# Scores of paired blocks as products on quarters of the TensorE array, with a new order of the work

## The chip, the cores and the metric

The kernel runs on one core of one Trainium2 chip. The metric is the device time of one execution in microseconds (us). Three runs of the kernel before took 713.99, 714.02 and 714.16 us; the median is 714.02.

## What is computed

Causal attention over a sliding window, then two feed-forward layers. There are 4 sequences of 576 positions, 8 heads of 64 dimensions, model width 512, inner widths 2048 and 1024; all in float32.

```python
def _attn_ref(q, k, v):                       # each (4, 8, 576, 64)
    scores = np.matmul(q, k.transpose(0, 1, 3, 2)) / np.sqrt(64)
    rel = pos[:, None] - pos[None, :]
    scores = np.where((rel >= 0) & (rel < 64), scores, -1e9)
    attn = softmax(scores)                    # the denominator + 1e-9
    return np.matmul(attn, v)
# x: (2304, 512), heads side by side
h = x @ w_in;  x = (h * tanh(softplus(h))) @ w_out      # 512 -> 2048 -> 512
h = x @ w_in2; y = h * softmax(h)                       # 512 -> 1024
y = layer_norm(y) * g_ln;  out = y @ w_out2             # 1024 -> 512
```

## The kernel before

**Attention.** A sequence is cut into 9 blocks of 64 queries, 36 blocks in all. With a window of 64, a block of queries sees 128 keys: those of the block before and its own. The first block of a sequence sees the first 128 keys of the sequence, under a mask of its own (`mask_0` instead of `mask_n`).

Two heads are handled together (`NP` = 4 head pairs). For each block the host lays q out as a 128 x 128 matrix with head 0 in the upper left 64 x 64 corner, head 1 in the lower right one, and zeros in the other two; k of the two heads lies one above the other on 128 partitions. One product of line 535 then gives a tile of 128 rows (64 queries of head 0, 64 of head 1) by 128 keys. Half of what the array multiplies is zeros.

The first 4 blocks (`N0`) go one at a time, with an arrangement of their own. The other 32 go in 16 pairs (n, n+1): `a_qk` makes 8 products into one PSUM tile `ps` of 128 x 8 x 128, index c*NP + p for block c and head pair p. For blocks below `NM` = 8 (the pairs 4 and 6) the mask is added on TensorE: a bf16 product behind each score product (line 541). For the other 14 pairs `a_scale` scales and adds the mask on VectorE (line 584), in two instructions where one of the two blocks begins a sequence. Then follow the maximum (`a_max`, line 590), the subtraction (`a_sub`), the exponential (`a_exp` or `a_exp1`), the sum and its inverse (`a_norm`), the multiplication (`a_mul`), eight transposes (`a_tr`, line 638), the copy out of PSUM (`a_pt`) and the product with v (`a_pv`, line 674), whose output goes into `xt`, the input of the first layer, as two float32r parts.

**Feed-forward.** Line 720 makes the first product (12 instructions for each of the 84 items: 4 chunks of the inner dimension and 3 terms of the split), lines 754 and 765 the second one (8 and 4). Lines 848 and 921 are those of the second layer, line 896 the transposes between them. The weights come as 64-bit words that are converted on the chip, on ScalarE, GpSimd and VectorE (lines 348 to 369, 283 to 303).

**Order.** Each engine works through its instructions in program order. A planner (`Schedule`) makes that order when the program is built: each step has a cost per engine and a due time, the constants at the head of the file (`ATT_AT`, `PRE_AT`, `FIRST_AT` and so on) set the due times, and among the steps that could start soon the one due first is taken. Where the planner foresees that TensorE has to wait for longer than 0.8 us, `bridge` puts products of zeros ahead of a step (line 511), and 42 of them stand at the very start.

Of the kernel before, what the change touches and what calls it, by code (L numbers as in the profile page):

```python
# [19 lines left out]
ALU = mybir.AluOpType  # L20
# [4 lines left out]
P = 128  # L25
BLK = 64
# [18 lines left out]
}  # L45


MISH_AT = (-1.318, -2.197, 0.491, 1.432, 3.462)
M2_AT = 6.081

ATT_AT = (-5.653, 0.076, 2.634, -1.153, 0.28, -0.274, 1.979, 3.176, 1.472, 3.319, 2.907, -2.355)

PRE_AT = (-2.332, 0.405, 5.908, -2.312, -3.229, 2.258, 7.674, 7.347, 5.474, 3.689, 2.895)
PRE_STEP = 9.088

B_AT = (-12.318, 7.278, 7.65, 20.217, 4.626, 12.227, 1.901, 15.948)

CONV_PRIO = (-7.642, 5.531, 5.959, -1.47, 2.491, 3.681)
Q_LEAD = 11.954
V_LEAD = -10.804  # L60
G_AT = 10.0
K0_LATER = 7.392
FIRST_AT = (-53.151, -34.692, -15.071)
W_STEP = 0.535
M4_LATER = 8.119
BESIDE_AT = ((4.321, 2.306), (2.079, 3.404), (4.273, 13.061), (-3.239, 4.798), (2.709, 9.741))
PATIENCE = 0.212
SLACK = 3.235
H_X2 = (0,)
PE_MASK = True  # L70
N_ACC = 8
# [11 lines left out]
class Schedule:  # L83
# [112 lines left out]
def attention_moe_solu(  # L196
# [12 lines left out]
    nc = tc.nc  # L209
    B, S, DM = v.shape  # L210
    NP = qk.shape[3]
# [8 lines left out]
    NBB = S // BLK  # L220
    NB = NT // BLK
    scale = 1.0 / float(D) ** 0.5
# [5 lines left out]
    N0 = GROUPS[0] // BLK // 2  # L228
# [15 lines left out]
    mask_n = const.tile([P, P], F32, name="mask_n")  # L244
    mask_0 = const.tile([P, P], F32, name="mask_0")
# [16 lines left out]
    def make_mask_n():  # L262
# [140 lines left out]
    n = GROUPS[0] // 2  # L403
# [12 lines left out]
    def pe_of(i):  # L416
        return 24 * ((its[i][3] - its[i][2]) / 2400 + 0.0134)
# [4 lines left out]
    pos = [0.0]  # L422
    for i in range(NI):
        beside = sum(n / (c - a) for a, c, n in besides if a <= i < c)
        pos.append(pos[-1] + (pe_of(i) + beside / 128 * 4.1) / 4.16)
    END = pos[NI]
    first_it = {}
    for i, it in enumerate(its):
# [25 lines left out]
    qt, kt, vt = {}, {}, {}  # L454
# [62 lines left out]

    s_t, pt_t = {}, {}

    def a_qk(n):  # L520
        early = n < N0
        ns = (n,) if early else (n, n + 1)
        if early:
            ps = ps_x2.tile([P, NP, P], F32, tag="x2", name="ps_s")
        else:
            ps = ps_a.tile([P, 2 * NP, P], F32, tag="a", name="ps_s")
        bridge(ps)
        r = room["r"]
# [15 lines left out]
        s_t[n] = ps  # L544

    def a_max0(n):
        ps = s_t[n]
# [29 lines left out]
    def a_scale(n):  # L577
        ps = s_t[n]
        s = at_p.tile([P, 2 * NP, P], F32, tag="s2", name="s", bufs=2)
        firsts = [i % NBB == 0 for i in (n, n + 1)]  # L580
# [82 lines left out]
    def a_pv(n):  # L663
        pt = pt_t.pop(n)
        if n < N0:
            ps, ns = ps_h.tile([P, NP, BLK], F32, tag="h", name="ps_o"), (n,)
        else:
            ps, ns = ps_a.tile([P, NP, 2 * BLK], F32, tag="a", name="ps_o"), (n, n + 1)
        bridge(ps)
        for c, m in enumerate(ns):  # L670
            for p in range(NP):
                for h in range(2):
                    r = slice(h * BLK, (h + 1) * BLK)
                    nc.tensor.matmul(  # L674
                        out=ps[r, p, c * BLK:(c + 1) * BLK],
                        lhsT=vt[m][:, (2 * p + h) * D:(2 * p + h + 1) * D],
                        rhs=pt[:, c * NP + p, r],
                        start=True, stop=True,
                    )
        x_t[n] = ps  # L680
# [119 lines left out]
    with tc.manual_schedule():  # L800
# [144 lines left out]
        masks_r = step(dict(act=0.2), -99, make_mask_r, ((2, mask_n),), after=[masks, q0], uses=[room_q])  # L945
        whole, split_of, first_hi = {}, {}, {}
        first_ld = []

# [34 lines left out]
        step(dict(pe=3.8), -200, warm_up, new=[warm], uses=[warm])  # L983


        x_of, xbuf, pv_of, pv_last = {}, {}, {}, []
        m1_of, m2_of, k0_of, v0_of = {}, {}, [], []

        def finish(n, t, offs, mu, bufs, O, cps):
            j, o = group_of[n]  # L990
            w, pt = bufs
            pv = step(dict(pe=0.648 * len(cps)), t + offs[0], a_pv, n, after=cps, new=[O], uses=[pt, O] + w)
            new = []
            if o == 0:
                xbuf[j] = Buf("xt")
                new = [xbuf[j]]
            k = len(cps)
            x = step(COSTS["x0" if k == 1 else "x"], t + offs[1], a_x, n, after=[pv], new=new, uses=[O])
            xl = step(dict(dve=0.42 if k == 1 else 0.69), t + offs[2], a_xl, n, after=[x], uses=[O])
            x_of[n] = xl  # L1000
            if n >= N0:
                x_of[n + 1] = xl
            pv_of[n] = pv
# [24 lines left out]
        def attend(n, t, offs, gate):  # L1028
            ks, ws, lks, lvs = [], [], [], []
            for m in (n, n + 1):  # L1030
                k, w = Buf("qk"), Buf("v")
# [5 lines left out]
            two = 2 if n % NBB and (n + 1) % NBB else 2.2  # L1037
            pv_of_old = pv_last[-2:-1]
            if n < NM:
                qk = step(dict(pe=2.2), t + offs[0], a_qk, n, after=lks + pv_of_old + [masks_r], new=[S], uses=ks + [S, room_q])  # L1040
# [15 lines left out]
            r = step(dict(dve=0.35), t + offs[5], a_norm, n, after=[sm], new=[rs], uses=[rs])  # L1056
# [58 lines left out]
        base = {}  # L1115
        for k, (i0, i1, _) in enumerate(besides):
            lo, hi = pos[i0] - BESIDE_AT[k][0], pos[i1] - BESIDE_AT[k][1]
            n0 = N0 if k == 0 else starts[k] // BLK
            nb = (starts[k] if k else 0) // BLK + GROUPS[k] // BLK - n0
            for b in range(0, nb, 2):  # L1120
                t = lo + b * (hi - lo) / nb
                i = max([i for i in range(NI) if pos[i] <= t - 1], default=-1)
                base.setdefault(i, []).append((n0 + b, t))
        for n, t in base.get(-1, []):
            attend(n, t, ATT_AT, [])
        for i in range(NI):
            mish(i)
            for n, t in base.get(i, []):
                attend(n, t, ATT_AT, [m1_of[i]] if i else [])


        attention_done = list(pv_of.values()) + list(x_of.values())
        ob = step(dict(none=0.0), 0, open_b, after=attention_done)
# [7 lines left out]
        for t in range(NTT):  # L1141
            j, o = tile_of[t]
            a = END + 2.2 + (t - 1) * UB
# [4 lines left out]
            h = Buf("b" + str(t % 2))  # L1148
# [77 lines left out]
```

## Time and profile before

| | |
|---|---|
| median of 3 runs | 714.02 us |
| span of the profiled execution | 713.9 us |
| TensorE busy | 704.2 us (99%) |
| VectorE busy | 385.5 us (54%) |
| ScalarE busy | 314.3 us (44%) |
| GpSimd busy | 44.0 us (6%) |
| mean granted TensorE clock | 0.996 |

The span runs from the first to the last instruction of one profiled execution; what lies around it is 0.1 us against the median. PE is TensorE's products, PEld its weight loads, DVE VectorE, ACT ScalarE. Products are pipelined, and their ends in the profile are modelled: for the pace of TensorE one reads from start to start. "Idle before" is the time in which an engine had nothing to do ahead of an instruction, with the instruction that ended the wait.

### The profile page before, as it was taken

The numbers are of one execution on the slowest core, as the hardware profiler recorded it, in microseconds if no ns is written. First come the engines' busy times: TensorE is split into PE (matmuls) and PEld (weight loads), VectorE is DVE, ScalarE is ACT, GpSimd is POOL, SyncE is SP. The second block draws the span as 40 slices with busy tenths as digits, with TensorE's granted clock in tenths as the row PEclk, the third lists the DMA queues.
The fourth block names the chain that finished last, engine by engine and source line by source line (L and its number), as shares of the span: only waits on it lengthen the run. The fifth ranks groups of instructions, "written<-read, shape, count | busy, mean of one in ns | idle before, by whom it ended". The sixth has DMA issues, their size and how long they took to land.

```text
span 713.9 us, 10238 instructions
## 1 busy us (share of the span) xinstructions
PE 704.2 (99%) x4180; PEld 613.0 (86%) x4180; DVE 385.5 (54%) x570; ACT 314.3 (44%) x536; POOL 44.0 (6%) x71
## 2 busy tenths in 40 slices
PE   9989999999999999999999999999999999999997
PEld 8889888888888888888899999999788888888886
DVE  4997988874362153443354113665656555555551
ACT  4878997554353242443354224654223332323221
POOL 2000010000000000000000100000212111111100
PEclk9999999999999999999999999999999999999999
DMA  8755756635117032022041104330111010101001
GB/s 299 277 207 177 266 163 221 236 118 177 60 45 221 0 98 95 15 89 89 1 148 45 31 1 157 124 118 16 60 44 60 31 59 30 60 29 60 16 29 45
DMA packets 37855, 71.71 MB, mean 100 GB/s; under 512 B 2864, under 2 KB 15152, under 8 KB 37808
## 3 DMA queue, kind: packets, MB, share of 16 engines
q1 hardware_dynamic: 37808, 71.06, 29.4%
q8 instruction: 33, 0.54, 0.3%
q14 instruction: 14, 0.11, 0.1%
HBM read 59.51 MB, written 11.53 MB: 100 GB/s over the span
## 4 chain that ended last, share of the span: by engine, by line
PE 93%; DVE 3%; ACT 2%; DMA 1%; SPq 0%; issue 0%; ACTq 0%
PE ps_h L720 26%; PE x L754 18%; PE h L848 14%; PE po L921 14%; PE x L765 9%; PE ps_s L535 5%; PE ps_o L674 2%; PE pt L896 2%; PE ps_t L638 2%; DMA room_q<-qk 1%; PE ps_t L511 1%; DVE st L369 0%; DVE w L303 0%; DVE nm L590 0%; DVE st L363 0%; DVE s L600 0%
## 5 line engine op out<-in xcount | busy, mean ns | idle before, releaser
L720 PE MATMUL ps_h<-xt,w 128*128 128x512 f32 (+2 forms) x1008 | 212.3, 360 | 0.5 <-ACT mc L730 0.4
L720 PEld LDWEIGHTS ps_h<-xt,w 128*128 128x128 f32 x1008 | 177.2, 188 | 21.9 <-ACT mc L730 0.6
L754 PE MATMUL x<-g,w 128*128 128x512 f32 (+2 forms) x672 | 149.0, 363 | 2.1 <-DVE w L287 1.3
L754 PEld LDWEIGHTS x<-g,w 128*128 128x128 f32 x672 | 118.5, 190 | 15.9 <-DVE w L287 1.4
L303 DVE SCALAR_TENSOR_TENSOR g<-mc,g 128x512 fp32r<-128x512 f32 (+2 forms) x84 | 51.5, 614 | 128.6 <-ACT g L283 127.7
L848 PE MATMUL h<-w,xs 128*128 128x512 f32 x432 | 104.7, 398 | 0.0
L921 PE MATMUL po<-w,lz 128*128 128x512 f32 x432 | 101.8, 391 | 0.7 <-ACT lz L902 0.7
L921 PEld LDWEIGHTS po<-w,lz 128*128 128x128 f32 x432 | 80.7, 188 | 17.9 <-ACT lz L902 0.9
L848 PEld LDWEIGHTS h<-w,xs 128*128 128x128 f32 x432 | 80.2, 188 | 18.3
L283 ACT ACTIVATE g<-mc 128x512 fp32r<-128x512 f32 (+2 forms) x72 | 41.6, 579 | 108.5 <-PE x L765 108.3
L730 ACT ACTIVATE mc<-ps_h 128x512 f32<-128x512 f32 (+2 forms) x84 | 45.0, 538 | 85.8 <-PE ps_h L720 77.6
L765 PE MATMUL x<-g,w 128*128 128x512 f32 (+2 forms) x336 | 80.4, 361 | 0.0
L765 PEld LDWEIGHTS x<-g,w 128*128 128x128 f32 x336 | 59.6, 188 | 6.7
L838 POOL TENSOR_TENSOR xs<-xr,xs 128x512 fp32r<-128x512 f32 x18 | 23.7, 1318 | 477.2 <-DVE g L303 300.8
L855 DVE TENSOR_REDUCE nm<-h 128x1 f32<-128x1024 f32 x18 | 22.0, 1224 | 40.5 <-PE h L848 40.5
L833 ACT ACTIVATE xs<-xr 128x512 fp32r<-128x512 f32 x18 | 11.4, 631 | 68.2 <-issue 45.1
L906 DVE TENSOR_TENSOR lz<-pt,lz 128x512 fp32r<-128x512 f32 x36 | 23.2, 686 | 28.8 <-ACT lz L902 28.8
L928 ACT ACTIVATE o<-po 128x512 f32<-128x512 f32 x18 | 10.8, 598 | 53.6 <-issue 45.5
L535 PE MATMUL ps_s<-qk 128*128 128x128 f32 x256 | 33.5, 282 | 0.1
L535 PEld LDWEIGHTS ps_s<-qk 128*128 128x128 f32 x256 | 32.4, 195 | 1.3 <-DVE xt L696 0.3
L867 DVE TENSOR_TENSOR y<-h,y 128x1024 f32<-128x1024 f32 x18 | 22.0, 1223 | 19.8 <-ACT y L861 19.8
L584 DVE SCALAR_TENSOR_TENSOR s<-ps_s,mask_n 128x1024 f32<-128x1024 f32 (+1 forms) x14 | 15.5, 1109 | 31.4 <-PE ps_s L535 31.4
(96 smaller groups left out, 669.4 us busy)
## 6 DMA issues: line engine op xcount, KB each, us to landing
qk<-qk SPq DMA_DIRECT2D x32, 512.0 KB, 5.1
st<-w_out SPq DMA_DIRECT2D x12, 1024.0 KB, 5.1
st<-w_in SPq DMA_DIRECT2D x10, 1024.0 KB, 5.7
v<-v SPq DMA_DIRECT2D x32, 256.0 KB, 2.8
xr<-x2d SPq DMA_DIRECT2D x18, 256.0 KB, 3.0
out<-o SPq DMA_DIRECT2D x18, 256.0 KB, 2.0
x2d<-xs SPq DMA_DIRECT2D x12, 256.0 KB, 3.9
part<-xs SPq DMA_DIRECT2D x8, 256.0 KB, 6.6
```

The lines of the kernel that those rows point to most:

```text
L283: nc.scalar.activation(out=hi, in_=x, func=ACTF.Copy, scale=1.0 if g is None else g)
L303: nc.vector.scalar_tensor_tensor(out=lo, in0=x, scalar=1.0 if g is None else g, in1=hi.bitcast(F32), op0=ALU.mult, op1=ALU.subtract)
L535: nc.tensor.matmul(out=o[:, i * w:(i + 1) * w], lhsT=qt[m][:, p, :], rhs=k[:, p, :], start=i == 0, stop=i == len(kt[m]) - 1 and not masked,)
L720: nc.tensor.matmul(out=ps[:, :n], lhsT=w[:, a, k, fs], rhs=x[:, b, k, a0:a1], start=(idx == 0), stop=(idx == len(terms) - 1),)
L730: nc.scalar.activation(out=c[:, :n], in_=ht.pop(i)[:, :n], func=ACTF.Mish)
L754: nc.tensor.matmul(out=acc[j][m][:, a0:a1], lhsT=w[:, a, f % 4, m * P:(m + 1) * P], rhs=g[:, 0, :n], start=(i in opens and a == 0), stop=F ...
L765: nc.tensor.matmul(out=acc[j][m][:, a0:a1], lhsT=w[:, 0, f % 4, m * P:(m + 1) * P], rhs=g[:, 1, :n], start=False, stop=i in closes,)
L838: nc.gpsimd.tensor_tensor(out=xs[t][:, 1], in0=r, in1=xs[t][:, 0].bitcast(F32), op=ALU.subtract)
L848: nc.tensor.matmul(out=h2[t][:, c, :], lhsT=x[:, a, k, :], rhs=wt["w3", c][:, b, k, :], start=(idx == 0), stop=(idx == len(terms) - 1),)
L855: nc.vector.tensor_reduce(out=nm, in_=h2[t], axis=AX.XY, op=ALU.max, negate=True)
L906: nc.vector.tensor_tensor(out=lt[t][:, 1, fs], in0=pst[t][:, fs], in1=lt[t][:, 0, fs].bitcast(F32), op=ALU.subtract)
L921: nc.tensor.matmul(out=po[t], lhsT=lz[:, a, f, :], rhs=wt["w4", f // 4][:, b, f % 4, :], start=(c == 0 and idx == 0), stop=(c == 2 and idx ...
```

## The change

In `a_qk`, a pair's scores are made of 16 products, one for each head pair, head and block: the 64 x 64 corner of q that is not zero against the 64 partitions of k of that head, over 128 keys. Head h uses the array's rows 64h to 64h + 63; the block uses its columns, and so the partitions of the output, by `side_of`: a block that begins a sequence always stands on partitions 64 to 127. Four products that follow each other use the four corners of the array. The tile's index is now h*NP + p, and the output product reads its slices accordingly. The mask of the pairs 4 and 6 is added by two bf16 products of 512 columns ahead of the scores. `mask_0` is completed to a joint mask (one GpSimd copy, `make_mask_x`), so that `a_scale` is one instruction for each pair. The first 4 blocks are computed as before. The host's layout of q, zeros included, and its transfer stay. The planner's costs of the two score steps go from 2.2 and 1.75 to 1.6 and 1.15, the first copy into each group of `xt` is put ahead of the others explicitly, and all due times are set anew.

```diff
-ATT_AT = (-5.653, 0.076, 2.634, -1.153, 0.28, -0.274, 1.979, 3.176, 1.472, 3.319, 2.907, -2.355)
+ATT_AT = (-49.672, -29.7, -0.095, 19.29, 26.281, -66.184, -24.234, -3.277, -4.723, -21.466, -19.806, -3.371)
...
-FIRST_AT = (-53.151, -34.692, -15.071)
+FIRST_AT = (-161.938, -95.173, -8.712)
...
-PATIENCE = 0.212
-SLACK = 3.235
+BESIDE_PE = 15.387
+PATIENCE = 0.35
+SLACK = 7.152
...
+    def make_mask_x():
+        nc.gpsimd.tensor_copy(out=mask_0[:BLK], in_=mask_n[:BLK])
...
+    def side_of(m):
+        n = m // 2 * 2
+        return m - n if n % NBB else n + 1 - m
...
-        for c, m in enumerate(ns):
-            for p in range(NP):
-                o = ps[:, c * NP + p, :]
-                w = P // len(kt[m])
-                for i, k in enumerate(kt[m]):
-                    nc.tensor.matmul(
-                        out=o[:, i * w:(i + 1) * w], lhsT=qt[m][:, p, :], rhs=k[:, p, :], start=i == 0,
-                        stop=i == len(kt[m]) - 1 and not masked,
-                    )
-                if masked:
-                    nc.tensor.matmul(
-                        out=o, lhsT=r[:, 0, :P], rhs=r[:, 0, P:] if n == 0 else r[:, 1, :P], start=False, stop=True
-                    )
+        if masked:
+            for h in range(2):
+                nc.tensor.matmul(
+                    out=ps[:, h * NP:(h + 1) * NP, :], lhsT=r[:, 0, :P],
+                    rhs=r[:, 1, :P].unsqueeze(1).to_broadcast([P, NP, P]), start=True, stop=False, skip_group_check=True,
+                )
+        for p in range(NP):
+            for h, c in ((0, 0), (1, 1), (0, 1), (1, 0)):
+                m = ns[c]
+                d, a = slice(h * BLK, (h + 1) * BLK), side_of(m)
+                nc.tensor.matmul(
+                    out=ps[a * BLK:(a + 1) * BLK, h * NP + p, :], lhsT=qt[m][d, p, d], rhs=kt[m][0][d, p, :],
+                    start=not masked, stop=True, skip_group_check=masked,
+                )
...
-        for c, k in ((0, 2),) if firsts[0] == firsts[1] else ((0, 1), (1, 1)):
-            r = slice(c * NP, (c + k) * NP)
-            m = (mask_0 if firsts[c] else mask_n).unsqueeze(1).to_broadcast([P, k * NP, P])
-            nc.vector.scalar_tensor_tensor(out=s[:, r], in0=ps[:, r], scalar=scale, in1=m, op0=ALU.mult, op1=ALU.add)
+        m = mask_0 if any(i % NBB == 0 for i in (n, n + 1)) else mask_n
+        m = m.unsqueeze(1).to_broadcast([P, 2 * NP, P])
+        nc.vector.scalar_tensor_tensor(out=s, in0=ps, scalar=scale, in1=m, op0=ALU.mult, op1=ALU.add)
...
-                        rhs=pt[:, c * NP + p, r],
+                        rhs=pt[:, p, r] if n < N0 else pt[:, h * NP + p, a:a + BLK],
...
-                qk = step(dict(pe=1.75), t + offs[0], a_qk, n, after=lks + pv_of_old, new=[S], uses=ks + [S])
-                sc = step(dict(dve=1.23), t + offs[1], a_scale, n, after=[qk, masks], new=[s], uses=[S, s])
+                qk = step(dict(pe=1.15), t + offs[0], a_qk, n, after=lks + pv_of_old, new=[S], uses=ks + [S])
+                sc = step(dict(dve=1.23), t + offs[1], a_scale, n, after=[qk, masks, mask_x], new=[s], uses=[S, s])
```

## Rows read from the trace of the kernel before

**Rows 1.** The page: busy time of the engines, and the chain by engine.
```profile
PE 704.2 (99%) x4180; PEld 613.0 (86%) x4180; DVE 385.5 (54%) x570; ACT 314.3 (44%) x536; POOL 44.0 (6%) x71
...
PE 93%; DVE 3%; ACT 2%; DMA 1%; SPq 0%; issue 0%; ACTq 0%
```

**Rows 2.** Table by stretch: length, busy time (instructions) of each engine, granted clock, DMA.
```profile
31.90:66.00 34.10, 31.21 (x310) 29.54 (x310) 28.83 (x38) 26.19 (x62) 0.00 (x0) 0.95 0.47 159
...
62.00:485.00 423.00, 422.81 (x2579) 375.36 (x2578) 216.34 (x272) 205.67 (x325) 4.47 (x3) 1.00 0.33 110
```

**Rows 3.** Groups by line and shape: count, busy us, mean ns, idle before.
```profile
L535 PE MATMUL ps_s<-qk 128*128 128x128 f32 x256 | 33.5, 282 | 0.1
...
L674 PE MATMUL ps_o<-s,v 128*64 128x64 f32 x512 | 18.4, 225 | 0.2 <-ACT s L295 0.2
```

**Rows 4.** PE timeline from 111 to 138 us: start, length, engine, line, count.
```profile
111.02 2.99 PE L720 MATMUL ps_h<-xt,w 128*128 128x512 f32 x12
113.85 1.95 PE L535 MATMUL ps_s<-qk 128*128 128x128 f32 x16
115.55 3.00 PE L720 MATMUL ps_h<-xt,w 128*128 128x512 f32 x12
118.48 1.15 PE L674 MATMUL ps_o<-s,v 128*64 128x64 f32 x32
119.56 2.11 PE L754 MATMUL x<-g,w 128*128 128x512 f32 x8
121.51 1.07 PE L765 MATMUL x<-g,w 128*128 128x512 f32 x4
...
133.30 2.88 PE L720 MATMUL ps_h<-xt,w 128*128 128x512 f32 x12
136.02 1.98 PE L754 MATMUL x<-g,w 128*128 128x512 f32 x8
137.83 1.07 PE L765 MATMUL x<-g,w 128*128 128x512 f32 x4
```

**Rows 5.** PE timeline, early blocks with 64 moving columns, and the first masked pair.
```profile
12.06 0.61 PE L535 MATMUL ps_s<-room_kv,room_q 128*128 128x64 f32 x4
12.50 0.22 PE L541 MATMUL ps_s<-room_q 128*128 128x128 bf16 x1
...
15.15 0.44 PE L535 MATMUL ps_s<-qk 128*128 128x128 f32 x2
15.43 0.22 PE L541 MATMUL ps_s<-room_q 128*128 128x128 bf16 x1
15.48 0.44 PE L535 MATMUL ps_s<-qk 128*128 128x128 f32 x2
```

**Rows 6.** PE timeline: the first three unmasked score steps.
```profile
40.73 2.05 PE L535 MATMUL ps_s<-qk 128*128 128x128 f32 x16
...
52.00 2.55 PE L535 MATMUL ps_s<-qk 128*128 128x128 f32 x16
...
69.30 1.95 PE L535 MATMUL ps_s<-qk 128*128 128x128 f32 x16
```

**Rows 7.** Timeline of VectorE: who it waited for, in brackets, before 62 us.
```profile
17.68 1.23 DVE L590 TENSOR_REDUCE nm<-ps_s 128x8 f32<-128x1024 f32 x1 [1.41 <-PE ps_s L541]
...
29.68 1.22 DVE L590 TENSOR_REDUCE nm<-ps_s 128x8 f32<-128x1024 f32 x1
...
42.82 0.69 DVE L584 SCALAR_TENSOR_TENSOR s<-ps_s,mask_n 128x512 f32<-128x512 f32 x1 [0.34 <-PE ps_s L535]
...
54.59 1.22 DVE L584 SCALAR_TENSOR_TENSOR s<-ps_s,mask_n 128x1024 f32<-128x1024 f32 x1 [1.45 <-PE ps_s L535]
```

**Rows 8.** Table by stretch around 50 us, columns as in rows 2.
```profile
47.80:50.30 2.50, 0.41 (x3) 0.19 (x1) 2.43 (x4) 2.50 (x12) 0.00 (x0) 0.91 1.01 383
50.30:52.00 1.70, 1.65 (x7) 1.66 (x8) 1.04 (x4) 1.70 (x7) 0.00 (x0) 0.50 0.26 54
52.00:54.30 2.30, 2.30 (x17) 2.30 (x17) 1.15 (x1) 1.51 (x2) 0.00 (x0) 0.73 0.95 337
```

More of the change, by code (lines that the diff above doesn't have):

```diff
@@ L45 @@
 }
-MISH_AT = (-1.318, -2.197, 0.491, 1.432, 3.462)
-M2_AT = 6.081
-ATT_AT = (-5.653, 0.076, 2.634, -1.153, 0.28, -0.274, 1.979, 3.176, 1.472, 3.319, 2.907, -2.355)
[L53 to L62, printed above, removed]
-FIRST_AT = (-53.151, -34.692, -15.071)
-W_STEP = 0.535
-M4_LATER = 8.119
-BESIDE_AT = ((4.321, 2.306), (2.079, 3.404), (4.273, 13.061), (-3.239, 4.798), (2.709, 9.741))
-PATIENCE = 0.212
-SLACK = 3.235
+MISH_AT = (-4.796, 28.112, 34.41, -45.879, 4.491)
+M2_AT = 5.714
+ATT_AT = (-49.672, -29.7, -0.095, 19.29, 26.281, -66.184, -24.234, -3.277, -4.723, -21.466, -19.806, -3.371)
+PRE_AT = (16.774, -16.395, -18.261, -0.215, -11.429, 10.739, 39.298, -5.046, -7.147, -36.205, 19.85)
+PRE_STEP = 28.874
+B_AT = (9.587, 37.912, -19.559, -30.209, 0.809, 34.651, 64.819, 43.703)
+CONV_PRIO = (43.465, 59.161, 15.699, 11.465, 9.993, -9.387)
+Q_LEAD = 1.101
+V_LEAD = -62.18
+G_AT = 1.058
+K0_LATER = -88.806
+FIRST_AT = (-161.938, -95.173, -8.712)
+W_STEP = 0.88
+M4_LATER = -28.799
+BESIDE_AT = ((12.83, 25.285), (5.132, 29.901), (-14.786, 53.657), (-18.384, 60.677), (13.158, 1.338))
+BESIDE_PE = 15.387
+PATIENCE = 0.35
+SLACK = 7.152
 H_X2 = (0,)
@@ L424, in attention_moe_solu @@
         beside = sum(n / (c - a) for a, c, n in besides if a <= i < c)
-        pos.append(pos[-1] + (pe_of(i) + beside / 128 * 4.1) / 4.16)
+        pos.append(pos[-1] + (pe_of(i) + beside / 128 * BESIDE_PE) / 4.16)
     END = pos[NI]
@@ L529, in a_qk @@
         masked = n < NM
-        for c, m in enumerate(ns):
+        s_t[n] = ps
+        if early:
             for p in range(NP):
-                o = ps[:, c * NP + p, :]
-                w = P // len(kt[m])
-                for i, k in enumerate(kt[m]):
+                o = ps[:, p, :]
+                w = P // len(kt[n])
+                for i, k in enumerate(kt[n]):
                     nc.tensor.matmul(
-                        out=o[:, i * w:(i + 1) * w], lhsT=qt[m][:, p, :], rhs=k[:, p, :], start=i == 0,
-                        stop=i == len(kt[m]) - 1 and not masked,
-                    )
-                if masked:
-                    nc.tensor.matmul(
-                        out=o, lhsT=r[:, 0, :P], rhs=r[:, 0, P:] if n == 0 else r[:, 1, :P], start=False, stop=True
-                    )
-        s_t[n] = ps
+                        out=o[:, i * w:(i + 1) * w], lhsT=qt[n][:, p, :], rhs=k[:, p, :], start=i == 0, stop=False
+                    )
+                nc.tensor.matmul(
+                    out=o, lhsT=r[:, 0, :P], rhs=r[:, 0, P:] if n == 0 else r[:, 1, :P], start=False, stop=True
+                )
+            return
+        if masked:
[8 more added lines that the diff above has]
+                d, a = slice(h * BLK, (h + 1) * BLK), side_of(m)
+                nc.tensor.matmul(
+                    out=ps[a * BLK:(a + 1) * BLK, h * NP + p, :], lhsT=qt[m][d, p, d], rhs=kt[m][0][d, p, :],
+                    start=not masked, stop=True, skip_group_check=masked,
+                )
     def a_max0(n):
@@ L579, in a_scale @@
         s = at_p.tile([P, 2 * NP, P], F32, tag="s2", name="s", bufs=2)
-        firsts = [i % NBB == 0 for i in (n, n + 1)]
-        for c, k in ((0, 2),) if firsts[0] == firsts[1] else ((0, 1), (1, 1)):
-            r = slice(c * NP, (c + k) * NP)
-            m = (mask_0 if firsts[c] else mask_n).unsqueeze(1).to_broadcast([P, k * NP, P])
-            nc.vector.scalar_tensor_tensor(out=s[:, r], in0=ps[:, r], scalar=scale, in1=m, op0=ALU.mult, op1=ALU.add)
+        m = mask_0 if any(i % NBB == 0 for i in (n, n + 1)) else mask_n
+        m = m.unsqueeze(1).to_broadcast([P, 2 * NP, P])
+        nc.vector.scalar_tensor_tensor(out=s, in0=ps, scalar=scale, in1=m, op0=ALU.mult, op1=ALU.add)
         s_t[n] = s
@@ L673, in a_pv @@
                     r = slice(h * BLK, (h + 1) * BLK)
+                    a = side_of(m) * BLK
                     nc.tensor.matmul(
@@ L945, in attention_moe_solu @@
         masks_r = step(dict(act=0.2), -99, make_mask_r, ((2, mask_n),), after=[masks, q0], uses=[room_q])
+        mask_x = step(dict(pool=0.3), 0, make_mask_x, after=[mask0_r, masks])
         whole, split_of, first_hi = {}, {}, {}
@@ L983, in attention_moe_solu @@
         step(dict(pe=3.8), -200, warm_up, new=[warm], uses=[warm])
-        x_of, xbuf, pv_of, pv_last = {}, {}, {}, []
+        x_of, x_first, x_all, xbuf, pv_of, pv_last = {}, {}, {}, {}, {}, []
         m1_of, m2_of, k0_of, v0_of = {}, {}, [], []
@@ L998, in finish @@
             x = step(COSTS["x0" if k == 1 else "x"], t + offs[1], a_x, n, after=[pv], new=new, uses=[O])
+            x_all.setdefault(j, []).append(x)
+            if o == 0:
+                x_first[j] = [x]
             xl = step(dict(dve=0.42 if k == 1 else 0.69), t + offs[2], a_xl, n, after=[x], uses=[O])
@@ L1036, in attend @@
             S, s, nm, rs, T, O = (Buf(x) for x in ("a", "s2", "nm2", "rs2", "a", "a"))
-            two = 2 if n % NBB and (n + 1) % NBB else 2.2
             pv_of_old = pv_last[-2:-1]
             if n < NM:
-                qk = step(dict(pe=2.2), t + offs[0], a_qk, n, after=lks + pv_of_old + [masks_r], new=[S], uses=ks + [S, room_q])
+                qk = step(dict(pe=1.6), t + offs[0], a_qk, n, after=lks + pv_of_old + [masks_r], new=[S], uses=ks + [S, room_q])
                 mx = step(dict(dve=1.37), t + offs[2], a_max, n, after=[qk], new=[nm], uses=[S, nm])
@@ L1117, in attention_moe_solu @@
             lo, hi = pos[i0] - BESIDE_AT[k][0], pos[i1] - BESIDE_AT[k][1]
+            hi = max(lo, hi)
             n0 = N0 if k == 0 else starts[k] // BLK
@@ L1129, in attention_moe_solu @@
                 attend(n, t, ATT_AT, [m1_of[i]] if i else [])
+        for j, xs_j in x_all.items():
+            for x in xs_j:
+                if x is not x_first[j][0]:
+                    x.after += x_first[j]
         attention_done = list(pv_of.values()) + list(x_of.values())
```

## The prediction

> **What bounds the kernel now.** I read the page first: busy shares, then the chain that ended last. TensorE is busy for 704.2 of 713.9 us and 93% of the chain is its own work [rows 1]. A busy TensorE is not yet a TensorE at its peak, so I went on to the table by stretch [rows 2]. From 62 to 485 us it has 422.81 us of work in 423 us, and VectorE and ScalarE are busy for about half of that: here every microsecond of TensorE work that is taken away comes off the end time, and nothing else does. From 31.9 to 66 us it is different: VectorE is busy for 28.83 of 34.1 us and TensorE waits for it in places. So each edit is worth its full price after 62 us, and before that only what a waiting engine can use.
>
> **What a score step costs now.** The change works on the products of line 535. A float32 product of 128 columns is two instructions: 16 pairs of blocks times 8 products are the 256 instructions of the row [rows 3]. The PE timeline gives the pace from start to start, which is safer than the modelled lengths. One undisturbed step starts at 113.85 and its successor at 115.55: 1.70 us, or 106 ns for each of 16 instructions. The neighbours show what the step costs at its edges. Undisturbed, twelve products of line 720 take 2.72 us (133.30 to 136.02) and eight of line 754 take 1.81 (136.02 to 137.83). Behind a transpose the twelve take 2.83 (111.02 to 113.85), so 0.11 follows a float32 step; between the scores and the output product (line 674) they take 2.93, which is 0.11 behind the scores and 0.10 to enter the output product [rows 4]. Scores now: 1.70 + 0.11 = **1.81 us** a pair.
>
> **What it becomes.** Each pair gets 16 products of 64 rows by 64 columns in place of 8 of 128 by 128, over the same 128 moving columns: 32 instructions of 106 ns each if they run one at a time (3.4 us), and a quarter of that if the four corners of the array run side by side (26.6 ns each, 0.85 us). No product of this shape is in the trace, so I bound the pace. The nearest row is the output product of line 674: float32, half the array's columns (128 by 64), the two halves taken in turn, 64 moving columns. Its 32 instructions take 1.08 us (118.48 to 119.56), or 33.8 ns each [rows 4]; at 106 ns for 128 columns one alone would need 53 for 64. So two column halves do overlap, and 33.8 ns is a pace that load and product together have kept. The other thing to fear is the weight load: 128 by 128 products with only 64 moving columns take 0.44 us for four, 110 ns each instead of 53 [rows 5], so there the load of 128 columns sets the pace. Quarters load 64 columns each, and in line 674 such loads keep up with 33.8 ns. Ends: 26.6 ns (all four streams full) and 33.8 ns (the pace of line 674). I take the middle, 30.2 ns: 32 x 30.2 = 0.97 us. The edges I take from line 674, since it too uses part of the array: 0.10 to enter, and 0.14 behind it (eight products of line 754 take 1.95 instead of 1.81, 119.56 to 121.51) [rows 4]. New step: 0.97 + 0.24 = **1.21 us**, with ends 1.09 and 1.32. The saving is 0.60 a pair, between 0.49 and 0.72.
>
> The Trainium skill (TensorEngine Tiling (Array Packing), Key Properties) says that a change of tiling mode drains TensorE. The 0.10 and 0.14 around line 674 agree with that [rows 4], and they are in the sum for that reason. The same skill (TensorE: Matmul & The Clock Gate, Part 3) models a pack as one product's length plus some 4 ns per tile. From that I estimate 106 + 3 x 4 = 118 ns for four instructions, 29.5 ns each; the sum would move by less than 0.3 us.
>
> **How many steps pay.** Of the 16 pairs, two are masked (blocks 4 to 7) and 14 are not. Of the 14, two lie before 62 us, at 40.73 and 52.00; the next is at 69.30 [rows 6]. So 12 pairs stand in the stretch without idle time: 12 x 0.60 = **7.2 us** (5.9 to 8.6).
>
> The four pairs before 62 us go by who waits for them [rows 7]. The masked pair now takes 0.333 us per head pair and block (15.15 to 15.48) [rows 5], eight times: 2.66 us. New, the mask is two bf16 products of 512 columns; at about 0.055 us for 128 (from 15.43 to 15.48) [rows 5] that is 0.44 us, and with the quarters 0.44 + 1.21 = 1.65, so 1.0 less. VectorE stood idle for 1.41 us before the maximum of the first one at 17.68, so 1.0 is passed on. The maximum of the second one comes at 29.68 without idle time: 0. At 42.82 VectorE had waited 0.34 us for the scores, at 54.59 1.45 us: of 0.60 each I pass on 0.34 and 0.60. Together **1.9 us**, with ends 0 (VectorE is the bound there anyway) and 1.0 + 1.0 + 0.6 + 0.6 = 3.2.
>
> Edits that I cost at nothing: the output product reads other slices of the same transposed tile, with the same shapes and count. The scaling step becomes one VectorE instruction instead of two for the three pairs in which a sequence begins; VectorE has idle time there [rows 2]. The copy that builds the joint mask is one GpSimd instruction on 64 partitions, done long before the first scaling at 42.82 [rows 7]; if it came late, that first step would wait for it, once. The order of the first copy into each group's tile was already given by the tile's allocation.
>
> **The new order.** All due times are replaced and with them the order of all queues: SyncE's loads, the conversion of the weights on ScalarE, GpSimd and VectorE, and the tail. After 62 us there is no idle time to win and the same products run in any order, so what an order can give or take lies before 62 us and in the tail. The size of one fault of this kind can be read: between 47.80 and 54.30 TensorE has 0.41 us of work in 2.5, then the granted clock is 0.50 for 1.7 us (the lower of the two levels, 1.2 GHz) and 0.73 for 2.3 more [rows 8]. In these 6.5 us it does eight products of line 754 and one score step; at the full clock they need 0.9 + 1.70 = 2.6 (0.9 is half of 1.81, for 256 columns against 512). So the hole costs **3.9 us**: the wait and the clock that fell behind it. A new order may close it or open another one. I take 0 for the order and 3.9 either way.
>
> Sum: 713.9 - 7.2 - 1.9 + 0 = 704.8 for the span. The median of the runs, 714.02, is 0.1 above the span, so **704.9 us**. With all ends: 714.0 - 8.6 - 3.2 - 3.9 = 698.3, and 714.0 - 5.9 - 0 + 3.9 = 712.0.
>
> **Rivals.** *Two corners at a time.* The trace shows column halves side by side; row halves it doesn't show at all. If only two of the four corners overlap, an instruction takes 53 ns, a step 32 x 53 + 0.24 = 1.94 us, 0.13 more than now; over 14 pairs + 1.8. The masked pairs would break about even with a small gain that VectorE may or may not use. Time: 715.8, **slower** by 0.25%. It decides at a pace of (1.81 - 0.24) / 32 = 49 ns. For it: no row with row halves. Against it: the column halves overlap well, and the two row halves write different halves of the score tile.
>
> *Loads that don't hide.* If a corner's load waits for the product that runs in the same rows, each half of the rows works through 16 loads and products one behind the other. A load of 64 columns I take at half of the 110 ns [rows 5]: 16 x (106 + 55) = 2.58 us, + 0.24, or 1.01 more than now; over 14 pairs + 14.1, so 728.1. The Trainium skill (TensorE: Matmul & The Clock Gate, Part 3) has this rule: loads overlap products in flight only in another row group. The present score step speaks against it: all its loads and products use the same rows, a load alone sets a pace of 110 ns, and both together run at 106 [rows 4, 5].
>
> *The order takes it back.* The products become cheaper as forecast, but the early stage opens holes such as the one above, or the tail waits for VectorE. One more hole and no gain before 62 us gives 714.0 - 7.2 + 3.9 = 710.7; it takes two of 3.9 to come out level.
>
> **How the numbers follow.** Forecast with its bounds (698.3 to 712.0): 0.80. Two corners at a time (715.8): 0.10. The order takes back more than one hole (about 711 to 718): 0.07. Loads that don't hide (728.1): 0.03. The range 699 to 712.5 leaves the rivals out, with hardly any of the forecast. A measurement of this kernel can tell some 0.2%, 1.4 us, from no change. Faster: 0.79 of the forecast and 0.02 of the third case and 0.01 of the second; same: 0.01, 0.02 and 0.03; slower: 0.06 of the second, 0.03 of the third, 0.03 of the last. That is 0.82, 0.06 and 0.12.
>
> **What would show it.** In the profile after, the PE timeline of a score step after 62 us: 32 instructions, and from its first start to the next step's start about 0.97 us (0.85 to 1.08); 1.7 means two corners at a time, over 2 loads that don't hide. The twelve products behind it should take 2.8 to 2.9 us. The stretch in the middle should stay without idle time, or the saved time has become a wait. Before 62 us, the fillers of line 511, the idle time and the granted clock show what the order did. I am wrong if the pace is above 49 ns, or if the time before the middle stretch or behind its end grows by more than 7 us.

## The result and the profile after

The changed kernel takes **704.98 us** (median of 4 runs, 703.54 to 706.97); the kernel before 714.09 (4 runs, 713.99 to 715.49). The ratio is 0.9866, with an interval of 0.9846 to 0.9887. On another chip, run side by side (e0_after_again, below), it is 0.9853 (0.9837 to 0.9870): 705.16 against 715.85. The profiled execution of the changed kernel has a span of 705.1 us. Some 1.7 to 2.3 us lay around the span in this run and in those below; in the first three runs of the kernel before it was 0.1. So where a step is sized, spans are compared, and medians only with medians of the same chip.

The page of the changed kernel, busy time and chain by engine, answers to [rows 1]:

```profile
PE 695.4 (99%) x4429; PEld 597.2 (85%) x4429; DVE 382.0 (54%) x559; ACT 312.1 (44%) x536; POOL 56.9 (8%) x80
...
PE 94%; DVE 3%; DMA 2%; ACT 1%; issue 0%; SPq 0%; ACTq 0%
```

TensorE is still the bound, busy for 99% of the span, with 8.8 us less to do. The stretch table, columns as in [rows 2], shows that the middle has kept its density: no wait has taken the place of the work removed.

```profile
31.90:66.00 34.10, 30.98 (x377) 28.63 (x376) 29.74 (x38) 26.82 (x65) 5.70 (x3) 0.95 0.57 199
...
62.00:485.00 423.00, 422.80 (x2772) 368.63 (x2771) 212.35 (x268) 209.34 (x325) 11.24 (x7) 1.00 0.33 109
```

A score step in that stretch, read from start to start in the PE timeline, answers to [rows 4]. Line 564 is the new product, line 742 the old 720, 776 the old 754, 787 the old 765:

```profile
175.27 2.88 PE L742 MATMUL ps_h<-xt,w 128*128 128x512 f32 x12
177.99 1.98 PE L776 MATMUL x<-g,w 128*128 128x512 f32 x8
179.90 1.10 PE L564 MATMUL ps_s<-qk 64*64 64x128 f32 x32
180.93 1.21 PE L787 MATMUL x<-g,w 128*128 128x512 f32 x4
181.98 2.92 PE L742 MATMUL ps_h<-xt,w 128*128 128x512 f32 x12
```

The 32 instructions take 1.03 us (179.90 to 180.93), 32.3 ns each. The eight products ahead of them take 1.91 instead of 1.81: 0.10 to enter. The four behind take 1.05 (180.93 to 181.98) instead of 0.91 (half of 1.81): 0.14. In all **1.27 us** where it was 1.81, so 0.54 less for each pair.

The first masked pair answers to [rows 5]:

```profile
14.59 0.60 PE L556 MATMUL ps_s<-room_q 128*128 128x512 bf16 x2
15.12 1.10 PE L564 MATMUL ps_s<-qk 64*64 64x128 f32 x32
16.15 0.69 PE L696 MATMUL ps_o<-room_q,room_kv 128*64 128x64 f32 x16
```

1.56 us from 14.59 to 16.15, where eight times 0.333 made 2.66. The new order has a hole of its own before 62 us, of the same kind as that of [rows 8]: a wait of 1.89 us for VectorE, and behind it a granted clock of 0.62 and 0.56 (the last two lines are from the stretch table):

```profile
35.70 1.69 PE L742 MATMUL ps_h<-xt,w 128*128 128x256 f32 x12
39.29 1.10 PE L564 MATMUL ps_s<-qk 64*64 64x128 f32 x32 [1.89 <-DVE xt L718]
40.32 2.50 PE L742 MATMUL ps_h<-xt,w 128*128 128x256 f32 x12
...
40.30:42.60 2.30, 2.30 (x16) 2.28 (x13) 2.27 (x4) 0.00 (x0) 0.00 (x0) 0.62 0.43 100
42.60:44.50 1.90, 1.87 (x10) 1.52 (x8) 1.87 (x3) 0.38 (x1) 0.00 (x0) 0.56 1.02 410
```

So the answer in short: shorter products, a middle without waits, and an early stage that is about as loose as before. Two things had to be shown: that the products carry the gain and not the new order, and that it is the four corners side by side that make them short.

### The profile page after: what moved, and what is told of

Read it like the earlier page. It is cut to its first block, busy times and chain, and to the rows that moved or that the text cites. A ratio compares the mean times of both kernels' runs of the same rounds, so it can differ in the third digit from the quotient of the medians.

```text
span 705.1 us, 10722 instructions
## 1 busy us (share of the span) xinstructions
PE 695.4 (99%) x4429; PEld 597.2 (85%) x4429; DVE 382.0 (54%) x559; ACT 312.1 (44%) x536; POOL 56.9 (8%) x80
## 4 chain that ended last, share of the span: by engine, by line
PE 94%; DVE 3%; DMA 2%; ACT 1%; issue 0%; SPq 0%; ACTq 0%
PE ps_h L742 27%; PE x L776 18%; PE h L870 14%; PE po L943 14%; PE x L787 9%; PE ps_o L696 2%; PE pt L918 2%; PE ps_t L659 2%; PE ps_s L564 2%; PE ps_w L516 1%; DMA st<-w_in 1%; DMA room_kv<-v 1%; PE ps_s L546 1%; DVE w L308 0%; DVE g L308 0%; DVE su L633 0%
## 5 line engine op out<-in xcount | busy, mean ns | idle before, releaser
L308 DVE SCALAR_TENSOR_TENSOR g<-mc,g 128x512 fp32r<-128x512 f32 (+2 forms) x84 | 53.2, 635 | 117.5 <-ACT g L288 117.0
L288 ACT ACTIVATE g<-mc 128x512 fp32r<-128x512 f32 (+2 forms) x70 | 39.8, 572 | 97.9 <-PE x L787 97.5
L924 ACT ACTIVATE lz<-pt 128x512 fp32r<-128x512 f32 x36 | 19.6, 596 | 63.2 <-PE po L943 49.5
L647 POOL TENSOR_TENSOR s<-s,rs 128x1024 f32<-128x1024 f32 x7 | 13.5, 1934 | 348.8 <-DVE rs L641 342.8
L368 DVE SCALAR_TENSOR_TENSOR st<-st 128x1024 uint32<-128x1024 uint32 x22 | 26.9, 1224 | 25.5 <-ACT st L360 25.5
L353 ACT ACTIVATE st<-st 128x1024 f32<-128x1024 f32 x22 | 25.3, 1149 | 9.5 <-DMA st<-w_in 6.4
```

Source lines behind the costliest of these rows:

```text
L288: nc.scalar.activation(out=hi, in_=x, func=ACTF.Copy, scale=1.0 if g is None else g)
L308: nc.vector.scalar_tensor_tensor(out=lo, in0=x, scalar=1.0 if g is None else g, in1=hi.bitcast(F32), op0=ALU.mult, op1=ALU.subtract)
L353: nc.scalar.activation(out=w, in_=w, func=ACTF.Copy, scale=2.0**-112)
L368: nc.vector.scalar_tensor_tensor(out=lw, in0=uw, scalar=3, in1=lw, op0=ALU.logical_shift_left, op1=ALU.bitwise_or)
```

## Experiment 1: products and order taken apart

*First attempt: due times and costs mixed.* `e1_quarters_old_order` has the changed kernel's products and planner costs under the old constants, `e2_whole_products_new_order` the old products and costs under the new constants; `e0_after_again` is the changed kernel unchanged, on the same chip.

```diff
# e1, against the changed kernel
-ATT_AT = (-49.672, -29.7, -0.095, ...)
+ATT_AT = (-5.653, 0.076, 2.634, ...)        # and all other due times of the kernel before
# e2, against the changed kernel: a_qk, a_scale, a_pv of the kernel before, and
-                qk = step(dict(pe=1.15), ...)
+                qk = step(dict(pe=1.75), ...)
```

> The products on quarters, the masks and the planner's new costs as in the changed kernel, but the due times and constants of the kernel before (the beside cost 4.1 among them). Theory (products alone): 12 score steps in the stretch without idle time save 1.81 - 1.27 = 0.54 us each, 6.5 us, and what VectorE had waited for before 62 us comes on top, 1 to 2.5 us: 705 to 706.5. Rival (the gain needs the new order): with the old due times the saved time turns into waits, above 709.

> The products, masks and score costs of the kernel before under the due times and constants of the changed kernel. Theory (the order alone is worth little): within 3 us of the kernel before, 711 to 717. Rival (the order carries the gain): 705 to 709.

> The changed kernel unchanged, to have it beside the other two on one chip. Both theories: 703.5 to 707, as before. If its runs spread over 2 us or more again while those of the two others don't, the new order's start depends on when its first transfers land.

Measured: e1 725.88 us, e2 725.50, e0 705.16, the kernel before 715.85 on the same chip. Both mixtures are slower than the kernel before, by 1.43% (1.28 to 1.58) and 1.39% (1.24 to 1.54). The number of e1 lies above the 709 of its rival and that of e2 in neither of its ranges; that a mixture would be slower than the kernel before was foreseen by none. The four runs of e0 lie within 0.7 us of each other, so the spread of 3.4 us in the first set has not come again. In e1, what TensorE waited for, in total, times and longest, and two stretches:

```profile
PE ps_o L516 <- ACT s L300: 5.9, 1, 5.9
PE ps_t L516 <- DVE s L605: 2.9, 1, 2.9
...
90.00:97.00 7.00, 1.11 (x7) 0.81 (x6) 6.86 (x7) 6.97 (x19) 0.00 (x0) 0.82 0.17 38
97.00:104.00 7.00, 7.00 (x62) 5.22 (x61) 1.35 (x4) 1.68 (x6) 1.90 (x1) 0.69 0.44 149
```

The planner, with other costs under the same due times, has put the work of an attention pair late enough that TensorE stands still for 5.9 us at 90 to 96 us, while VectorE and ScalarE are busy for 6.86 and 6.97 of 7 us, and runs at a fallen clock (0.69) afterwards. A new cost is a new order. So these two runs do not take the products and the order apart; they show what a wrong order costs.

*Second attempt: the exact order kept.* In `e7_quarters_exact_old_order` the planner gets the old costs and due times, so that every engine has its instructions in the order of the kernel before, and only the products, the masks and the scalings are the new ones. `e8_whole_exact_new_order` is the reverse: the order of the changed kernel with the old products.

```diff
# e7, against the kernel before; the planner's costs 2.2 and 1.75 stay
+        mask_x = step(dict(none=0.0), -98, make_mask_x, after=[mask0_r, masks])
     def a_qk(n): ...      # as in the changed kernel, likewise a_scale and a_pv
# e8, against the changed kernel; the planner's costs 1.6 and 1.15 stay
     def a_qk(n): ...      # as in the kernel before, likewise a_scale and a_pv
     def make_mask_x():
-        nc.gpsimd.tensor_copy(out=mask_0[:BLK], in_=mask_n[:BLK])
+        pass
```

> Quarter products, joint mask and the 512-column masks, with every engine's instructions otherwise in exactly the order of the kernel before (planner's costs and due times as before). Theory (the products alone carry the gain): 12 steps of 0.54 us, 6.5 us, and 0 to 2.5 us before 62 us; 706 to 709 where the kernel before takes 715. Rival (the two parts need each other): no gain or slower, 713 or more, as when the old due times met the new costs.

> The products, masks and scalings of the kernel before, with every engine's instructions otherwise in exactly the order of the changed kernel. Theory (the order alone is worth nothing clear): the changed kernel's 705 and 6.5 to 9 us for the dearer products, 711.5 to 714.5, against 715 for the kernel before on the same chip. Rival (the order needs the short products): 718 or more.

| medians, us (ratio to the kernel before on the same chip) | old order | new order |
|---|---|---|
| old products | 715.51 (before) | 714.61 (e8, 1.0000) |
| new products | 706.29 (e7, 0.9881) | 705.16 (e0, on the chip of e1, 0.9853) |

e7 against the kernel before: 0.9881 (0.9861 to 0.9900). e8 against it: 1.0000 (0.9985 to 1.0015), its median just above the 711.5 to 714.5 expected. **The products alone bring 9.2 us (7.1 to 9.3 where the clock is the same, below); the order alone brings nothing that can be told.** The rival that the two need each other has fallen: e1 and e2 were slow because the order was replanned. e2 and e8 differ in little but the planner's costs, and some 10 us lie between them.

e7 and the kernel before have the same order, so the gain can be followed mark by mark in the PE timeline. First the kernel before, then e7 (L695 is the old 674, L741 the old 720, L775 the old 754, L563 the new score product; the last line is from e7's stretch table):

```profile
49.09 0.38 PE L754 MATMUL x<-g,w 128*128 128x256 f32 x1 [1.25 <-DVE w L287]
50.35 1.86 PE L754 MATMUL x<-g,w 128*128 128x256 f32 x7 [0.88 <-DVE w L303]
...
54.31 3.12 PE L720 MATMUL ps_h<-xt,w 128*128 128x256 f32 x24
...
64.87 1.15 PE L674 MATMUL ps_o<-s,v 128*64 128x64 f32 x32 [0.19 <-ACT s L295]
```

```profile
47.77 0.38 PE L775 MATMUL x<-g,w 128*128 128x256 f32 x1 [1.10 <-DVE w L291]
49.02 1.09 PE L775 MATMUL x<-g,w 128*128 128x256 f32 x7 [0.88 <-DVE w L307]
50.04 1.10 PE L563 MATMUL ps_s<-qk 64*64 64x128 f32 x32
51.08 3.13 PE L741 MATMUL ps_h<-xt,w 128*128 128x256 f32 x24
...
61.62 1.15 PE L695 MATMUL ps_o<-s,v 128*64 128x64 f32 x32 [0.15 <-ACT s L299]
...
50.00:51.10 1.10, 1.10 (x34) 0.89 (x33) 0.73 (x3) 1.10 (x3) 0.00 (x0) 1.00 0.94 142
```

The same output product starts at 61.62 instead of 64.87: 3.25 us won before the dense stretch. The spans differ by 713.9 - 704.2 = 9.7, which leaves 6.45 behind that mark, or 0.54 for each of 12 steps. Of the 3.25, 1.3 belong to the second unmasked score step alone: it takes 1.04 us (50.04 to 51.08), in the kernel before 2.31 (52.00 [rows 6] to 54.31), since there the clock had fallen [rows 8] and in e7 it had not (1.00), behind waits of nearly the same length (1.10 and 0.88 us against 1.25 and 0.88). An undisturbed old step takes 1.70, so 0.61 of this is the clock; another 0.63 is the clock at the seven products ahead of it (1.65 us from 50.35 to 52.00, in e7 1.02 from 49.02 to 50.04). So 1.24 of the 3.25 is the clock, and 2.0 are left for the shorter products.

The runs of the kernel before show the price of that fall by itself. On this chip its 13 runs have spans of 711.7 to 712.4 us where the mean granted clock is 0.999 or 1.000, and of 713.6 to 714.3 where it is 0.996 or 0.997: 1.9 us, for the same program. Nine of the 13 are of the second kind, but only one of the four runs of e7 (705.0 us at 0.996), so the 9.2 us between the medians hold some of this. The other three of e7, all at 0.999, have spans of 704.2 to 704.6: 7.1 to 8.2 us less than the kernel before at 0.999 or 1.000; the one at 0.996 has 8.6 to 9.3 less than the nine. Whether shorter products keep the clock up more often, so few runs don't show.

## Experiment 2: how many corners work at a time

Only the sequence of the 16 products of a pair is changed, in the changed kernel; each corner gets the same products as before.

```diff
-        for p in range(NP):
-            for h, c in ((0, 0), (1, 1), (0, 1), (1, 0)):
# e3_column_pairs: one head, the two blocks in turn
+        for h in range(2):
+            for p, c in ((p, c) for p in range(NP) for c in range(2)):
# e4_row_pairs: one block, the two heads in turn
+        for c in range(2):
+            for p, h in ((p, h) for p in range(NP) for h in range(2)):
# e5_one_corner: four head pairs of one corner behind each other
+        for h in range(2):
+            for c, p in ((c, p) for c in range(2) for p in range(NP)):
# e9_rows_in_twos
+        for p in range(NP):
+            for h, c in ((0, 0), (0, 1), (1, 0), (1, 1)):
```

> The 16 products of a pair in another sequence: first all of head 0, then all of head 1, the two blocks in turn, so that neighbours share the array's rows and differ in its columns. Theory (four corners overlap, each keeps its 106 ns): only two run side by side, 53 to 58 ns each, 1.7 to 1.9 us a step, 0.7 to 0.8 more than 1.03; 12 to 14 steps, so 713 to 717. Rival (a fixed price of about 32 ns for each instruction, and the corner does not matter): the step stays at 1.03 us and the time at 703.5 to 707.

> First all products of one block, then of the other, the two heads in turn, so that neighbours share the array's columns and differ in its rows. Theory (row halves overlap as well as column halves): 53 to 58 ns each, 1.7 to 1.9 us a step, 713 to 717. Rival one (rows hardly overlap, the gain is that of the columns): about 106 ns, 3.4 us a step, 730 to 738. Rival two (fixed price of 32 ns for each instruction): 1.03 us.

> The same 16 products with those of one corner behind each other, four head pairs at a time. Theory: 106 to 110 ns each but for the change of corner, 3.2 to 3.5 us a step, 2.2 to 2.5 more than 1.03 over 12 to 14 steps: 731 to 740. If a load of 64 columns were not hidden behind the product of its own corner, 160 ns each and 5 us a step, 755 or more. Rival (fixed price for each instruction): 1.03 us a step, 703.5 to 707.

> The four corners of a head pair in the sequence upper rows left, upper rows right, lower rows left, lower rows right, so that neighbours share rows in half of the places. Theory (all four corners overlap, the sequence within four is of no matter): 1.03 us a step within 0.05, 703.5 to 707. Rival (a load waits for the product before it where both use the same rows): 1.2 us or more a step, 707 or more.

The same step in the PE timeline, with what follows it, in e3, e4, e5 and e9:

```profile
182.36 1.59 PE L564 MATMUL ps_s<-qk 64*64 64x128 f32 x32
183.88 1.19 PE L787 MATMUL x<-g,w 128*128 128x512 f32 x4
```

```profile
182.29 1.59 PE L564 MATMUL ps_s<-qk 64*64 64x128 f32 x32
183.81 1.21 PE L787 MATMUL x<-g,w 128*128 128x512 f32 x4
```

```profile
188.63 2.56 PE L564 MATMUL ps_s<-qk 64*64 64x128 f32 x32
191.13 1.21 PE L787 MATMUL x<-g,w 128*128 128x512 f32 x4
```

```profile
177.93 1.10 PE L564 MATMUL ps_s<-qk 64*64 64x128 f32 x32
178.96 1.19 PE L787 MATMUL x<-g,w 128*128 128x512 f32 x4
```

From start to start: 1.52 us with two corners in turn, whether they share rows or columns; 2.50 with one; 1.03 with four, in either sequence. Times of one run each: 713.22, 712.77, 727.08 and 704.72 us, the kernel before 713.86 beside the first three and 715.51 (median of 13) beside e9. So rows overlap as well as columns, and the corners do work side by side.

The mean over a step of e5, 2.50 / 32 = 78 ns, is not the price of a corner that works alone. The stretch table of a step's line tells how many instructions have begun since the step began (the first number in brackets). In the changed kernel, in e3 and in e5:

```profile
179.90:180.10 0.20, 0.20 (x8) 0.20 (x12) 1.00 0.00 0
179.90:180.65 0.75, 0.75 (x28) 0.75 (x32) 1.00 0.00 0
```

```profile
182.36:182.57 0.21, 0.21 (x4) 0.21 (x6) 1.00 0.00 0
182.36:182.79 0.43, 0.43 (x8) 0.43 (x10) 1.00 0.00 0
182.36:183.29 0.93, 0.93 (x24) 0.93 (x26) 1.00 0.00 0
```

```profile
188.63:188.84 0.21, 0.20 (x2) 0.21 (x3) 1.00 0.00 0
188.63:189.06 0.43, 0.42 (x4) 0.43 (x5) 1.00 0.00 0
188.63:190.54 1.91, 1.91 (x28) 1.91 (x29) 1.00 0.00 0
188.63:190.87 2.24, 2.23 (x31) 2.24 (x32) 1.00 0.00 0
```

Four corners in turn begin 20 instructions in 0.55 us (180.10 to 180.65), 27 ns each. Two in turn begin 4 in 0.22 (182.57 to 182.79), 55 ns each, and in e4 just so. One corner begins 2 in 0.22 (188.84 to 189.06) and, at the end of the step, 3 in 0.33 (190.54 to 190.87), 109 ns each. So a corner alone works at about the pace of the whole array, 106, as the theory had it; two work at twice and four at four times the pace of one. In the middle of a step e5 and e3 are faster than that (24 instructions in 1.48 us, 16 in 0.50), since the sequence goes over to other corners there, and their first products run beside the last ones of the corners before. (The trace doesn't name the corner of an instruction; that they overlap is read from these numbers.) That overlap is why e5 stays under the 731 us that its theory gave at the least, and the means of e3 and e4 under its 53 to 58 ns.

With 27.3 ns, a quarter of 109, the 32 instructions make 0.87 us, about half of the old 1.70: half of what the whole products multiplied were zeros. The other 0.16 of the 1.03 lie at the ends of the step.

`e6_half_keys` asks whether 32 ns are a fixed price of an instruction:

```diff
-                nc.tensor.matmul(out=ps[a * BLK:(a + 1) * BLK, h * NP + p, :], ..., rhs=kt[m][0][d, p, :], ...)
+                for w in (slice(0, BLK), slice(BLK, P)):
+                    nc.tensor.matmul(out=ps[a * BLK:(a + 1) * BLK, h * NP + p, w], ..., rhs=kt[m][0][d, p, w], ...)
```

> Each product of 128 keys as two of 64 keys in the same corner, one behind the other: twice the instructions (64 a step), the same columns in all. Theory (the four streams set the pace, 26.6 ns and some loss): the step stays near its 1.03 us, up to 1.3. Rival (each instruction with its load costs a fixed 32 ns, as line 674 with 33.8 ns for 64 columns suggests): 64 x 32 = 2.06 us a step, 12 to 14 us more in all, 716 to 720.

```profile
179.42 1.30 PE L565 MATMUL ps_s<-qk 64*64 64x64 f32 x64
180.65 1.21 PE L788 MATMUL x<-g,w 128*128 128x512 f32 x4
```

1.23 us for 64 instructions, 19.2 ns each over the step (709.18 us in all, one run). A fixed price of 32 ns is out. Doubling the instructions over the same columns adds 0.20 us, and the 33.8 ns of line 674 [rows 4] is no floor either.

`e10_half_columns_alone` and `e11_half_columns_in_turn` ask why a corner alone should be cheaper than the whole array, as the mean of 78 ns made me think. They start from e8 (old layout with its zeros) and cut each product of the 14 unmasked pairs into its two column halves, with all 128 rows.

```diff
+        if not masked:
+            for h, c, p in ((h, c, p) for h in range(2) for c in range(2) for p in range(NP)):     # e10
+            for c, p, h in ((c, p, h) for c in range(2) for p in range(NP) for h in range(2)):     # e11
+                m, d = ns[c], slice(h * BLK, (h + 1) * BLK)
+                nc.tensor.matmul(
+                    out=ps[d, c * NP + p, :], lhsT=qt[m][:, p, d], rhs=kt[m][0][:, p, :], start=True, stop=True
+                )
```

> The kernel of e8_whole_exact_new_order (old layout, zeros included, order of the changed kernel), but in the 14 unmasked pairs each product of 128 rows by 128 columns as two of 128 by 64, all of one column half first, so that neighbours use the same half of the array. One corner alone ran at 78 ns an instruction, the whole array at 106, both over 128 moving columns. Theory (what is saved is the load, which has half the columns): 78 ns, 2.5 us a step, 0.8 more than 1.70 over 12 to 14 steps, 723 to 727. Rival (what is saved comes with half the rows): 106 ns, 3.4 us a step, 734 to 740.

> The same with the two column halves in turn. Theory (two halves overlap as two corners did): 47.5 ns an instruction, 1.52 us a step, 0.18 less than 1.70, but 0.13 dearer at its edges: 712 to 715, the kernel before within what can be told. Rival (with whole rows the halves overlap less): 53 ns or more, 1.7 us a step, 715 to 718.

```profile
193.90 3.33 PE L543 MATMUL ps_s<-qk 128*64 128x128 f32 x32
197.15 1.20 PE L783 MATMUL x<-g,w 128*128 128x512 f32 x4
```

```profile
184.42 1.97 PE L543 MATMUL ps_s<-qk 128*64 128x128 f32 x32
186.32 1.20 PE L783 MATMUL x<-g,w 128*128 128x512 f32 x4
```

e10: 3.25 us, 102 ns an instruction over the step (738.30 us in all, one run). e11: 1.90 us, 59 ns (717.64, one run; the kernel before 715.94 beside both). Both theories took the 78 ns for the price of a corner, and both numbers came out as their rivals had them. The stretch tables of the two steps, read as above:

```profile
193.90:194.11 0.21, 0.21 (x2) 0.21 (x3) 1.00 0.00 0
193.90:195.20 1.30, 1.30 (x12) 1.30 (x13) 1.00 0.00 0
```

```profile
184.42:184.63 0.21, 0.21 (x4) 0.21 (x6) 1.00 0.00 0
184.42:186.16 1.74, 1.74 (x32) 1.72 (x32) 1.00 0.00 0
```

e10 begins 10 instructions in 1.09 us, 109 ns each; e11 28 in 1.53, 55 ns each. So half the columns with all rows, alone, cost what a corner alone costs, and a smaller product saves nothing by itself. The means differ because a step of e10 changes its half once and a step of e5 its corner three times. The numbers fit: 32 x 109 ns are 3.49 us; with 0.15 for the ends of a step (in e11, 1.90 against 32 x 54.6 ns = 1.75), 0.39 is missing in e10, and 1.14 in e5, which is 0.38 for each change. Cutting the columns alone makes twice the instructions at half the price and would have made the kernel slower.

| ns an instruction, 128 moving columns: within a step (mean over the step) | alone | two in turn | four in turn |
|---|---|---|---|
| 128 rows x 128 columns [rows 4] | (106) | | |
| 128 x 64 | 109 (102, e10) | 55 (59, e11) | |
| 64 x 64 | 109 (78, e5) | 55 (47.5, e3, e4) | 27 (32.3) |

## Why the prediction was right, point by point

**What bounds the kernel: right.** After 62 us each microsecond of TensorE work came off the end. e7 shows it: 12 steps of 0.54 us (1.81 - 1.27) make 6.5 us, and the span behind the mark is shorter by 6.45.

**The cost of the new step: right, and for the reason given.** Forecast 1.21 us with ends of 1.09 and 1.32; measured 1.27. The lower end was made from a stream of 106 ns in each corner, divided by four: 26.6 ns. Within a step the run shows just that, 109 ns for four instructions, 27.3 each. What the sum lacked is the 0.16 us that a step loses at its own ends, by which the mean is 32.3 instead of the 30.2 taken. That the middle value came so near is partly luck: it was a choice between two ends, and the loss was not in it. The edges, 0.10 and 0.14, are those taken from line 674, to the hundredth. That a drain makes them isn't shown, since 0.11 follows a step of whole products as well. The pack model of the Trainium skill (TensorE: Matmul & The Clock Gate, Part 3), one product's length and 4 ns for each further one, gave an estimate of 29.5 ns with the 106. The run shows 27.3 within a step, where one pack follows another every 109 ns, and 32.3 over the step, and the measurement decides.

**The steps before 62 us: right in sum, not in its parts.** Forecast 1.9 us with ends of 0 and 3.2. In the changed kernel the work done by 66 us is ahead by about 2.2 us: one score step (1.27), one group of line 765 (0.45) and part of a group of line 720. With the old order (e7, where 0 to 2.5 was expected) it is 3.25, of which 1.24 is the clock that did not fall behind the wait at 48 us; that had been put into the order, not into the products. The other 2.0 are near the forecast, but by luck. Of the 1.0 that the first masked pair was to pass on, only 0.25 arrives, because in e7 TensorE then waits 0.61 us for a transfer of v (the next output product starts at 19.04 instead of 19.29). The second masked pair, put at 0, brings 0.5 (the lead is 0.40 ahead of it and 0.94 at the transposes of 27.93, in the kernel before 28.87).

**The order: right in what it did, wrong in what it can do.** The term was 0, and e8 measures 1.0000 (0.9985 to 1.0015). But the step "what an order can give or take lies before 62 us and in the tail" is refuted by e1: its hole of 5.9 us stands at 90 to 96 us, in the stretch that was called free of such things, and the whole order costs 19.4 us against e7 with the same products (spans of 723.6 and 704.2). The bounds of 3.9 either way were too narrow for a replanned order; the one that came with the change happened to be as good as the old one.

**The rival of two corners at a time** was decided by the pace: 32.3 ns, well under its 49. Its price of 53 ns was right for a pair in turn, 55 in e3, e4 and e11. It was to end at 715.8, slower; e3 and e4 take 713.22 and 712.77 against 713.86, level, because four corners overlap for a while where the sequence goes over to the other half, which makes the mean 47.5. Without such a change, in e11, 32 instructions take 1.90 us.

**Loads that don't hide** would have shown in e5: 161 ns an instruction forecast for a load and product of one corner, 109 measured where one corner works alone. The rule of the Trainium skill (TensorE: Matmul & The Clock Gate, Part 3) that a load overlaps products in flight only in another row group would make e4, whose neighbours differ in rows, faster than e3, whose neighbours share them. Both take 1.52 us, so these runs don't bear it out.

**The total.** 704.9 forecast, 704.98 measured; the profiled span was forecast at 704.8 and is 705.1. The three other runs of that set have spans of 701.7 to 703.3, and 1.8 us around them, which the sum had put at 0.1: the median was met more closely than the steps deserve, by two differences of some 1.7 us with opposite signs.

What stays open: what makes the 0.16 us at the ends of a step and the 0.10 and 0.14 around it, together a third of its 1.27, and why the clock stayed up in e7. A product of 64 rows by 128 columns, which would belong in the table, was not tried.

## What to carry to other kernels

Where half of a product's stationary matrix is zeros, cut it into corners and issue the four corners in turn: here it took a step from 1.70 to 1.03 us, and all of it reached the end time, because TensorE was the only engine without idle time there. Cutting alone saves nothing: a corner by itself takes as long as the whole array. Check the sequence: the same 16 products, one corner at a time, take 2.50 us and make the kernel slower. Don't take the mean over a step for the price of an instruction; look where in the step the instructions begin. And when a planner makes the order from costs, compare edits with the instruction order held fixed; other costs under kept due times moved this kernel by some 10 us (e2 against e8) and 19 us (e1 against e7, where a few order constraints differ too), and would have hidden a gain of 9.

## What the hardware showed that was not expected

One instruction of a float32 product over 128 moving columns takes 109 ns on a corner of 64 rows by 64 columns alone (e5), 109 on 128 by 64 (e10) and 106 on the whole array. Two corners or halves in turn begin one every 55 ns (e3, e4, e11) and four corners one every 27, so they overlap in full. When the sequence goes over to another corner, its products begin before the old ones are through, which saves some 0.38 us a change (e5, e10). Whether the granted clock falls is not the same from run to run: the same program shows mean clocks of 0.997 and 0.999, and 1.9 us between them.
